# Routing calls of a pipeline step written behind the state update instead of ahead of it

## The chip, the cores and the metric

The kernel runs on one core of a Trainium2 chip. The metric is the device time of one execution, in microseconds. Engines are named as in the profile: PE (TensorE, matmuls and transposes), PEld (its weight loads), DVE (VectorE), ACT (ScalarE), POOL (GpSimd) and SP (SyncE, which issues most DMAs).

## What is computed

Two layers follow each other. The first is a linear attention with a decaying state, per batch and head; the second sends each token to one of eight experts. Cut to what matters, the reference is:

```
for t in range(S):                      # S = 768, head_dim 48, 4 batches, 8 heads
    state = alpha[t, :, None] * state + outer(k[t], v[t])
    y[t]  = q[t] @ state
x = y, one row per token                # 3072 tokens x 384
logits = x @ w_gate + modality_bias[modality_id]      # 8 experts
e_idx  = argmax(logits)
gate_w = softmax(logits)[e_idx]
for e in range(8):
    h = relu(x[e_idx == e] @ w1[e])     # 384 -> 1024
    out[e_idx == e] = gate_w * (h @ w2[e])            # 1024 -> 384
```

Which expert a token goes to is known only once its attention row exists; the kernel sorts the tokens by expert on the core and loads the weights of an expert once it knows that it is wanted.

## The kernel before, in words

**Attention as a pipeline.** The 3072 tokens are cut into 24 units of 128 (a batch has six). A unit passes through five steps of the loop over `s` (lines 797 to 845), and each pass of the loop works on five units at once: `turn_decay`, `decay` and `guard` on unit s, `scale_k` and `scale_q` on unit s-1, `keys` and `scores` on s-2, `combine` on s-3, `outputs`, `rows` and the logits on s-4. A pass is called a step below; there are 27.

`combine` (line 296) is the state's update. On PE it adds into one PSUM bank, tile `y`: the query times the old state (L324), the keys times the values (L330, which gives the new state's increment), and the masked scores times the values (L334). On DVE it then writes the new state S (L338, or L340 in the first unit of a batch), and in the next step the decayed state UB (L304). In the next step ACT copies the same bank out to `yt` (L347, `outputs`). PE needs `yt` for `logits_turned` (L369) and for `rows` (L357), whose result ACT copies to `xs` and SP stores to `xd` in DRAM.

**Routing beside it.** A dictionary `later` holds the routing functions for the step in which they are to be called. The units are taken in groups, `GROUPS = ((0, 6), (6, 12), (12, 16), (16, 18), (18, 22), (22, 24))`. For a group, `route_group` finds each token's expert (a one-hot tile `oh`) on DVE; `route_ranks`, one step later, counts on PE the place of each token within its expert (L453, L457, L461) and turns it into indices on DVE (L465 to L477). The calls fall into steps 10 and 11, 16 and 17, 20 and 21, 22 and 23, 25 and 26, and behind the loop. All of these PSUM results, and those of the logits, share one bank, tile `rt`, so that each waits until the one before has been read.

Two experts are begun early, before all tokens are routed. `route_early` (steps 22 and 24; L539, then L542 to L565) takes the expert with the most tokens so far, and writes its number to `meta` (L545) and a tile `OHE` (L554, L560); `weights` in the same step reads `meta` on SP and loads 3.1 MB of that expert's weights in four DMAs (L656, L658); `early` (steps 23 and 25) finds the tokens with small matmuls of `OHE` (L573), writes their indices (L528 to L533), and gathers their rows from `xd` with two indirect DMAs that POOL issues (L679). In step 25 PE transposes the first expert's gathered rows (`first_inputs`, L118), and from step 26 on it works on that expert's first layer (L111) between the last steps of the attention.

**What sets the order.** Each engine runs its own instructions strictly in the order in which they were put on it. From step 4 on every PE instruction of the loop is pinned to the order in which the Python code writes it (`pin`). On the other engines a scheduler chooses the order when the kernel is built, from what the code writes and its own estimate of when operands are ready; it may put an instruction ahead of one that was written earlier. SP's queue holds the row stores (L363) and the weight loads in one line, POOL's the masks of the scores (L282) and the indirect DMAs.

Behind the loop follow the experts, slot after slot, on PE almost without a pause (L925 to L950).

Of the kernel before, what the change touches and what calls it, by code (L numbers as in the profile page):

```python
# [54 lines left out]
def attention_moe(ctx: ExitStack, tc: tile.TileContext, q, k, v, alpha, mid, wg, mb, w1, w2, out):  # L55
# [49 lines left out]
    def first_layer(j, z, name="tr", bufs=3):  # L105

        if z == 0:
            hps.append(ps.tile([P, 2, T], F32, name=name, bufs=bufs))
        f = 256 * j + P * z
        for d in range(ND):  # L110
            pin(pe.matmul(hps[j][:, z], WR[0][0][:, d, f : f + P], xf[:, d], start=(d == 0), stop=(d == ND - 1)))  # L111

    def first_inputs():
        for d0, d1 in ((0, 2), (2, 3)):
            xp = ps.tile([P, d1 - d0, T], F32, name="sc", bufs=2)
            for d in range(d0, d1):
                for u in range(2):
                    pin(pe.transpose(xp[:, d - d0, u * P : (u + 1) * P], xg[0][:, u, d * P : (d + 1) * P], ident))  # L118
            act.copy(xf[:, d0:d1], xp)

    def pin(ins):

        if mark.get("pin"):
            tc.keep_in_program_order(ins)
        return ins

    def load(i, names="akqv"):
        b, c = divmod(i, NC)
        for n, t in (("a", alpha), ("k", k), ("q", q), ("v", v)):
            if n in names:  # L130
                dst = VT[i % NV][:, :, :D] if n == "v" else nat[n, i % NB][:, :, :D]
                sp.dma_start(dst, t[b, :, c * P : (c + 1) * P, :].rearrange("h t d -> t h d"))
# [97 lines left out]
    def turn_decay(i):  # L230
        pa = trans(i, "a")
        turned = (act.copy if i else vec.tensor_copy)(seg(X[i % 2][:, 1:], 0), pa)
        if i:
            mark["X"] = turned

    def decay(i):
        x, d = X[i % 2], DF[i % 2]
        Fw = sb.tile([P, NP * SEG], F32, name="Fw", bufs=3)
        G = sb.tile([P, NP * SEG + 1], F32, name="G", bufs=4)
        vec.tensor_tensor_scan(  # L240
            G[:, 1:][:, ::-1], x[:, 1:][:, ::-1], DR[:, 1:][:, ::-1], 0.0, op0=ALU.mult, op1=ALU.add
        )
        ac1 = amin[:, i]
        vec.tensor_scalar(ac1, G[:, 1::SEG], AFLOOR, None, op0=ALU.max)
        vec.reciprocal(d[:, 0::SEG], ac1)
        vec.tensor_tensor_scan(Fw, x[:, :-1], d, 0.0, op0=ALU.mult, op1=ALU.add)
        st[i, "G"], st[i, "F"] = G, Fw
# [11 lines left out]
    def scale_k(i):  # L259
        kh = sb.tile([P, NP, P], F32, name="kh", bufs=3)  # L260
        pk = trans(i, "k")
        vec.tensor_tensor(kh, pk, seg(st[i, "G"][:, 1:], 1), op=ALU.mult)
        st[i, "k"] = kh

    def scale_q(i):
        qh = sb.tile([P, NP, P], F32, name="qh", bufs=3)
        pq = trans(i, "q")
        vec.tensor_tensor(qh, pq, seg(st[i, "F"], 1), op=ALU.mult)
        st[i, "q"] = qh
# [15 lines left out]
    def keys(i):  # L285

        kh = st[i, "k"]
        if i % NC < NC - 1:
            p = ps.tile([P, NP, P], F32, name="tr", bufs=3)
            for j in range(NP):  # L290
                pin(pe.transpose(p[:, j], kh[:, j], ident))
            kn = sb.tile([P, NP, P], F32, name="knat")
            act.copy(kn, p)
            st[i, "n"] = kn

    def combine(i):
        c = i % NC
        qh, vt, sc = st[i, "q"], VT[i % NV], st[i, "s"]
        U = UB[i % 2]
        halves = [slice(64 * g, 64 * g + 64) for g in range(2)]  # L300
        if c > 0:
            S0 = st[i, "S"]
            A = st[i, "G"][:, 1::SEG].unsqueeze(2).broadcast_to([P, NP, D])
            vec.tensor_tensor(U[:, :, :D], S0, A, op=ALU.mult)  # L304

        yk = ps.tile([P, 2, 512], F32, name="y")

        def y(r, j):
            return yk[r, j % 2, P * (j // 2) : P * (j // 2 + 1)]

        kv = yk[:, 1, 2 * P : 2 * P + NP * D].rearrange("p (j d) -> p j d", j=NP)
        fresh = {(o, g) for o in range(2) for g in range(2)}

        def first(o, g):
            new = (o, g) in fresh
            fresh.discard((o, g))
            return new

        if c > 0:
            for a in range(2):  # L320
                for o in range(2):
                    for g in range(2):
                        x, j = g ^ o, 2 * a + o
                        pin(pe.matmul(y(halves[x], j), U[halves[g], j], qh[halves[g], j], start=first(o, x), stop=False))  # L324
        if c < NC - 1:
            kn = st[i, "n"]
            for h in range(H):
                j = h // 2
                r = halves[h % 2]
                pin(pe.matmul(kv[r, j], kn[:, j, r], vt[:, h, :D], start=first(1, h % 2), stop=False))  # L330
        for j in range(NP):
            for x, r in enumerate(halves):
                g = x ^ j % 2
                pin(pe.matmul(y(r, j), vt[:, 2 * j + g], sc[g][:, j], start=first(j % 2, x), stop=(j > 1)))  # L334
        if c < NC - 1:
            S1 = sb.tile([P, NP, D], F32, name="S")
            if c > 0:
                vec.tensor_tensor(S1, U[:, :, :D], kv, op=ALU.add)  # L338
            else:
                vec.tensor_copy(S1, kv)  # L340
            st[i + 1, "S"] = S1
        st[i, "yp"] = yk

    def outputs(i):
        yt = sb.tile([P, 2, NP, P], F32, name="yt") if i % 2 == 0 else st[i - 1, "yt"]
        with issue_after("X"):
            act.copy(  # L347
                yt[:, i % 2].rearrange("p (a o) t -> p o a t", o=2),
                st[i, "yp"][:, :, : 2 * P].rearrange("p o (a t) -> p o a t", a=2),
            )  # L350
        st[i, "yt"], st[i, "y"] = yt, yt[:, i % 2]
# [13 lines left out]
    def logits_turned(i):  # L365

        lt = ps.tile([P, 2, P], F32, name="rt")
        for j in range(NP):
            pin(pe.matmul(lt[32 * j : 32 * j + 32], wgp[:, j], st[i, "yt"][:, :, j], start=True, stop=True))  # L369
        l2 = sb.tile([P, 2, P], F32, name="lts")  # L370
        mark["lts"] = act.copy(l2, lt)
        st[i, "l"] = l2

    def logits(i):

        lp = ps.tile([P, 2, P], F32, name="rt")
        for c in range(2):
            pin(pe.transpose(lp[:, c], st[i, "l"][:, c], ident))
        z = slice(i - 1, i + 1)
        vec.tensor_reduce(L[:, z], lp.rearrange("p c (j e) -> p c e j", e=32)[:, :, :E], axis=AX.X, op=ALU.add)  # L380
# [389 lines left out]
    later = {}  # L770
# [26 lines left out]
    for s in range(NU + 3):  # L797
        mark["pin"] = s > 3
        if s > 0 and s + PF - 1 < NU:
            load(s + PF - 1)  # L800
        if s < NU:
            turn_decay(s)
        if 0 <= s - 4:
            outputs(s - 4)
        if s == NU + 1:
            first_inputs()
        if s == NU + 2:
            first_layer(0, 0, "sc", 2)
            first_layer(0, 1)
        if 0 <= s - 1 < NU:  # L810
            scale_k(s - 1)
        if 0 <= s - 1 < NU:
            scale_q(s - 1)
        if s < NU:
            decay(s)
        if 0 <= s - 2 < NU:
            keys(s - 2)
        if s > 4 and s % 2 == 0 and s <= NU:
            logits(s - 5)
        if s > 4 and s % 2:  # L820
            logits_turned(s - 4)
        if 0 <= s - 4:
            rows(s - 4)
        if 0 <= s - 2 < NU:
            scores(s - 2)
        for f, a in later.pop(s, ()):
            f(*a)
        if s < NU:
            guard(s)
        if s == 5:  # L830
            table = bias_table()
            next(table)
        if s == 6:
            next(table, None)
            half_index()
        if s == 4:
            sp.dma_start(xd[MID : MID + 1], zr)
            sp.dma_start(gd[MID : MID + 1], zr[:, 0:1])
        if s == NU:
            out_of_range()  # L840
        if 0 <= s - 3 < NU:
            combine(s - 3)
        if s == NU + 1:
            logits(s - 4)
            route_group(*GROUPS[-2])
# [239 lines left out]
```

## Time and profile before

| what | value |
|---|---|
| median of 3 runs | 410.47 us |
| the three runs | 410.47, 408.89, 410.51 us |
| the profiled execution's own time | 408.91 us |
| its span in the profile | 407.1 us |
| PE busy in the span | 378.2 us (93%) |
| DVE / ACT / POOL busy | 278.2 (68%) / 224.3 (55%) / 137.3 us (34%) |
| attention steps | to about 170 us; experts after that |

The view of waits names who waited for whom and for how long in all. The view by stretches gives the busy time of each engine between two moments, and at the end of its row the mean clock granted to PE (1.00 is full), the share of time in which the 16 DMA engines were busy, and GB/s. The timeline gives start and length in us, engine, line, operation and, in brackets, how long the engine had been idle and who released it; rows that carry one line number and follow each other are merged with their count. DMA queue q1 holds what SP issues, q0 what POOL issues.

### The profile page before, as it was taken

What the parts mean: (1) busy time and instruction counts of PE and PEld (TensorE: products, weight loads), DVE (VectorE), ACT (ScalarE), POOL (GpSimd) and SP (SyncE); (2) the same over time, 40 slices, a digit from 0 to 9 for tenths busy, and PEclk for the clock granted to TensorE, in tenths of its full rate; (3) what the DMA queues carried; (4) which work ended last, traced back from release to release, by engine and by line L of the source; (5) the groups of instructions that cost most, each with busy time, mean ns of one, the idle gap of its engine ahead of it and who ended that gap; (6) DMA issues with size and microseconds to landing.
All of it is one profiled execution on the core that took longest, in us unless ns stands there. A gap on an engine that the chain in (4) does not pass through costs nothing. (4 is left out here: it accounts for less than half of the span.)

```text
span 407.1 us, 9558 instructions
## 1 busy us (share of the span) xinstructions
PE 378.2 (93%) x3659; PEld 347.7 (85%) x3659; DVE 278.2 (68%) x550; ACT 224.3 (55%) x425; POOL 137.3 (34%) x175
## 2 busy tenths in 40 slices
PE   3898999999999888899997999999999999999992
PEld 3777787788778666778997999999999999999992
DVE  6787889878979965587689566665656666554230
ACT  3467677567566435344586657475654656545230
POOL 9321321321222233402657515244351634232010
PEclk9999999999999989999998999999999999999998
DMA  6999988579675096505999786566867657420010
GB/s 129 209 202 214 201 184 192 127 165 199 138 160 117 26 360 210 204 22 163 385 370 331 252 283 202 198 220 203 268 197 264 210 195 238 148 106 35 6 42 10
DMA packets 132655, 75.12 MB, mean 185 GB/s; under 512 B 103777, under 2 KB 120222, under 8 KB 132600
## 3 DMA queue, kind: packets, MB, share of 16 engines
q1 hardware_dynamic: 128504, 64.57, 56.6%
q0 software_dynamic: 4096, 9.85, 7.0%
q8 instruction: 31, 0.51, 0.5%
q14 instruction: 24, 0.20, 0.1%
HBM read 64.95 MB, written 9.65 MB: 183 GB/s over the span
## 5 line engine op out<-in xcount | busy, mean ns | idle before, releaser
L925 PE MATMUL tr<-xH,w1H 128*128 128x256 f32 x264 | 74.7, 286 | 1.3 <-DVE hL L932 1.3
L926 PE MATMUL tr<-xL,w1H 128*128 128x256 f32 x264 | 75.1, 285 | 0.0
L927 PE MATMUL tr<-xH,w1L 128*128 128x256 f32 x264 | 74.9, 285 | 0.0
L282 POOL TENSOR_SCALAR_AFFINE_SELECT scT<-scT 128x512 f32<-128x512 f32 x48 | 35.2, 754 | 107.1 <-ACT scT L281 107.1
L948 PE MATMUL sc<-w2H,hH 128*128 128x384 f32 x192 | 65.4, 342 | 1.0 <-ACT hH L929 1.0
L949 PE MATMUL sc<-w2L,hH 128*128 128x384 f32 x192 | 64.6, 337 | 0.0
L899 DVE TENSOR_TENSOR w2L<-w2r,w2H 128x768 fp32r<-128x768 f32 x52 | 49.1, 956 | 21.9 <-ACT w2H L897 21.0
L950 PE MATMUL sc<-w2H,hL 128*128 128x384 f32 x192 | 63.6, 340 | 0.0
L866 POOL DMA_INDIRECT out_dram<-os,odx x24 | 27.6, 1148 | 89.2 <-ACT os L953 34.9
L899 DVE TENSOR_TENSOR w1L<-w1r,w1H 128x768 fp32r<-128x768 f32 x44 | 41.7, 956 | 21.3 <-ACT w1H L897 20.6
L897 ACT CAST w1H<-w1r 128x768 fp32r<-128x768 f32 x44 | 36.0, 834 | 29.8 <-PE tr L926 23.0
L925 PEld LDWEIGHTS tr<-xH,w1H 128*128 128x128 f32 x264 | 50.9, 194 | 1.6 <-issue 1.6
L926 PEld LDWEIGHTS tr<-xL,w1H 128*128 128x128 f32 x264 | 51.2, 194 | 0.0
L927 PEld LDWEIGHTS tr<-xH,w1L 128*128 128x128 f32 x264 | 51.1, 194 | 0.0
L679 POOL DMA_INDIRECT xg<-xd,idx x26 | 32.0, 1230 | 42.5 <-PE y L887 36.5
L897 ACT CAST w2H<-w2r 128x768 fp32r<-128x768 f32 x52 | 42.2, 834 | 7.0 <-PE sc L950 6.8
L932 DVE SCALAR_TENSOR_TENSOR hL<-tr,hH 128x512 fp32r<-128x512 f32 x46 | 31.5, 686 | 10.5 <-ACT hH L929 7.2
L948 PEld LDWEIGHTS sc<-w2H,hH 128*128 128x128 f32 x192 | 36.1, 188 | 2.4 <-ACT hH L929 1.2
L929 ACT ACTIVATE hH<-tr 128x512 fp32r<-128x512 f32 x46 | 27.4, 595 | 16.2 <-PE tr L927 12.7
L684 POOL DMA_INDIRECT gg<-gd,idx x26 | 30.9, 1187 | 15.8 <-DMA gd<-gs 8.5
L949 PEld LDWEIGHTS sc<-w2L,hH 128*128 128x128 f32 x192 | 36.1, 188 | 0.0
L950 PEld LDWEIGHTS sc<-w2H,hL 128*128 128x128 f32 x192 | 36.0, 188 | 0.0
(218 smaller groups left out, 703.9 us busy)
## 6 DMA issues: line engine op xcount, KB each, us to landing
w1r<-in_moe_w_dram SPq DMA_DIRECT2D x26, 768.0 KB
w2r<-in_moe_w_dram SPq DMA_DIRECT2D x26, 768.0 KB
nat_a<-in_alpha_dram SPq DMA_DIRECT2D x24, 192.0 KB
nat_k<-in_k_dram SPq DMA_DIRECT2D x24, 192.0 KB
nat_q<-in_q_dram SPq DMA_DIRECT2D x24, 192.0 KB
vt<-in_v_dram SPq DMA_DIRECT2D x24, 192.0 KB
xd<-xs SPq DMA_DIRECT2D x24, 192.0 KB
xg<-xd,idx POOLq DMA_INDIRECT x26
```

Of the source, the lines that this page charges most:

```text
L282: pool.affine_select(s, s, [[0, NP], [1, P]], ALU.is_ge, 0.0, base=0, channel_multiplier=-1)
L679: pool.indirect_dma_start(xg[i % NX][:, u], None, xd[0:rows], ix, bounds_check=rows - 1, oob_is_err=False)
L684: pool.indirect_dma_start(gg[i % NX][:, u : u + 1], None, gd[0:rows], ix, bounds_check=rows - 1, oob_is_err=False)
L897: act.copy(hi, src)
L899: vec.tensor_tensor(lw, src, hi.bitcast(F32), op=ALU.subtract)
L925: pe.matmul(hp[:, z], wH[:, d, fs], xH[:, d], start=(d == 0), stop=False)
L926: pe.matmul(hp[:, z], wH[:, d, fs], xL[:, d], start=False, stop=False)
L927: pe.matmul(hp[:, z], wL[:, d, fs], xH[:, d], start=False, stop=(d == ND - 1))
L932: mark[f"h{j}L"] = vec.scalar_tensor_tensor(hL, hp, 0.0, hH.bitcast(F32), op0=ALU.max, op1=ALU.subtract)
L948: pe.matmul(op, hH[:, z, us], wH[:, z], start=(f == 0), stop=False)
L949: pe.matmul(op, hH[:, z, us], wL[:, z], start=False, stop=False)
L950: pe.matmul(op, hL[:, z, us], wH[:, z], start=False, stop=(f == NF - 1))
```

## The change

Two lines move within the loop's body. The call of the routing functions that are due in a step stood between `scores(s - 2)` and `guard(s)`; it now stands behind `combine(s - 3)`. Nothing is added or removed, and no function changes. (`route_ranks` of the last group, which puts ranks and counts into one tile, reads the same in both kernels; so do the calls behind the loop, and the explicit `route_group` of step 25.)

```diff
@@ -823,8 +823,6 @@
             rows(s - 4)
         if 0 <= s - 2 < NU:
             scores(s - 2)
-        for f, a in later.pop(s, ()):
-            f(*a)
         if s < NU:
             guard(s)
         if s == 5:
@@ -840,6 +838,8 @@
             out_of_range()
         if 0 <= s - 3 < NU:
             combine(s - 3)
+        for f, a in later.pop(s, ()):
+            f(*a)
         if s == NU + 1:
             logits(s - 4)
             route_group(*GROUPS[-2])
```

On DVE in step 11, the place where the ranks of the first group are turned into indices (L465 to L477), with the new state S of `combine` (L338), its decayed form (L304), the scaled keys (L262) and the scan of the decay (L240):

```order
+L338 TENSOR_TENSOR S<-UB_154,y 128x192
 L465 TENSOR_TENSOR rk<-rt,oh 128x48
 L473 TENSOR_TENSOR ohs<-ohs,hsum 128x8
+L304 TENSOR_TENSOR UB_160<-S,G 128x4x48
 L467 TENSOR_REDUCE r_209<-rk 128x6
 L474 TENSOR_SCALAR hr<-r_209 128x6
 L475 TENSOR_SCALAR lo<-r_209 128x6
+L262 TENSOR_TENSOR kh<-tr,G 128x512
 L476 SCALAR_TENSOR_TENSOR hi<-m_194,hr 128x6
+L240 SCALAR_TENSOR_TENSOR G<-X_150,DR 128x516
 L477 TENSOR_TENSOR OL<-ioh,lo 128x768
-L338 TENSOR_TENSOR S<-UB_154,y 128x192
```

S, which stood behind all seven routing operations, now stands ahead of the first; UB, the keys and the scan now stand among them. The same holds in steps 17 and 21. In steps 10, 16 and 20, where `route_group` runs, DVE's order does not change at all.

On DVE in step 22, from the reading of the counts for the first early expert (L542) to its number in `meta` (L545), on which SP's weight load waits (L436 to L438 belong to `route_group` of units 16 and 17):

```order
 L542 TENSOR_REDUCE base<-rt 128x1
-L436 SCALAR_TENSOR_TENSOR eq<-ls,rev 128x16
+L304 TENSOR_TENSOR UB_154<-S,G 128x4x48
 L543 SCALAR_TENSOR_TENSOR rest<-rt,base,rev 128x8
-L437 TENSOR_REDUCE m_194<-eq 128x2
+L262 TENSOR_TENSOR kh<-tr,G 128x512
 L544 TENSOR_REDUCE base<-rest 128x1
-L438 TENSOR_TENSOR oh<-eq,m_194 128x16
+L240 SCALAR_TENSOR_TENSOR G<-X_156,DR 128x516
+L268 TENSOR_TENSOR qh<-tr,Fw 128x512
 L545 TENSOR_SCALAR meta<-base 1x1
```

S of this step (L338) now stands directly ahead of L542, but behind `route_group`'s operations and three of the gates (L664 to L666). `meta`, which was written before S, is now written behind S, UB, the keys, the scan and the scaled queries (L268). `OHE` (L554, L560) moves further back still, behind the next scan (L246).

On PE in step 23, where the small matmuls find the tokens of the first early expert (L573):

```order
 L357 MATMUL tr<-ident,yt 128x128 x4
 L277 MATMUL sc<-qh,kh 128x128 x8
+L324 MATMUL y<-qh,UB_154 64x128 x8
+L330 MATMUL y<-vt_104,knat 64x48 x8
+L334 MATMUL y<-scT,vt_104 64x128 x8
 L573 LDWEIGHTS OL
 L573 MATMUL rt<-OHE,OL 128x2
```

The three products of `combine` come ahead of these matmuls and of the ranks that follow them (L453 to L461), instead of behind both and behind the transpose of the gates (L668). The same holds for the ranks and small matmuls in steps 11, 17, 21, 25 and 26. On POOL the gather of the first early expert moves behind both masks of step 23, where it stood between them; SP's order stays.

## The prediction

> **What bounds the kernel now.** I read the view by stretches first, one row for each step of the attention (from one step's L277 on PE to the next), with busy times, granted clock, DMA share and GB/s.
>
> ```profile
> 69.20:75.73 6.53, 6.23 (x95) 5.31 (x94) 6.39 (x16) 3.98 (x9) 1.57 (x2) 1.00 0.63 137
> ...
> 129.56:135.84 6.28, 5.61 (x77) 4.83 (x76) 6.14 (x16) 3.27 (x7) 1.59 (x2) 1.00 0.10 34
> 135.84:143.41 7.57, 6.54 (x94) 5.10 (x93) 7.54 (x30) 3.97 (x9) 1.84 (x2) 1.00 0.19 50
> 143.41:152.94 9.53, 7.83 (x104) 6.66 (x103) 6.47 (x26) 2.95 (x7) 3.88 (x4) 0.82 1.02 374
> 152.94:160.07 7.13, 5.79 (x86) 4.18 (x86) 4.10 (x18) 3.42 (x9) 3.24 (x4) 1.00 0.45 141
> 160.07:170.35 10.28, 9.21 (x139) 7.49 (x138) 5.34 (x23) 2.74 (x7) 5.30 (x6) 1.00 0.81 297
> 170.35:180.00 9.65, 9.65 (x61) 7.95 (x60) 5.97 (x13) 6.20 (x13) 0.00 (x0) 1.00 0.11 36
> ```
>
> PE (first pair behind the length) is the bound: from 170 us on it is full (last row). What can be gained is its idle time in the attention, and that lies in the steps with routing: steps 11 and 21 (first two rows), and above all 22 to 26 (the next four). One of these, step 23, also shows a granted clock of 0.82. The view of PE's waits in steps up to 26 says for whom it waits:
>
> ```profile
> PE rt L369 <- ACT yt L347: 3.7, 7, 1.0
> ...
> PE rt L453 <- DVE vals L529: 1.4, 1, 1.4
> PE tr L357 <- DVE kh L262: 1.4, 3, 0.8
> ...
> PE rt L453 <- issue: 1.1, 1, 1.1
> ...
> PE rt L703 <- DVE rest L543: 0.5, 1, 0.5
> ```
>
> Two kinds: PE waits for `yt` or kh, which come late because S is late on DVE behind routing; or for a routing operand with `combine`, ready to run, queued behind it. The timeline of steps 22 and 23 shows both:
>
> ```profile
> 137.13 0.67 PE L324 MATMUL y<-qh,UB 64*64 64x128 f32 x16
> ...
> 138.23 1.06 PE L334 MATMUL y<-scT,vt 128*64 128x128 f32 x16
> ...
> 139.04 0.56 DVE L436 SCALAR_TENSOR_TENSOR eq<-ls,rev 128x16 f32<-128x16 f32 x1
> ...
> 139.97 0.14 DVE L545 TENSOR_SCALAR meta<-base 1x1 int32<-1x1 f32 x1
> ...
> 141.12 1.01 SPq L656 DMA_DIRECT2D w1r<-in_moe_w_dram  x2
> ...
> 141.24 0.35 DVE L338 TENSOR_TENSOR S<-UB,y 128x192 f32<-128x192 f32 x1
> 141.62 0.59 ACT L347 COPY yt<-y 128x512 f32<-128x512 f32 x1 [1.06 <-DVE S L338]
> ...
> 142.26 0.64 PE L369 MATMUL rt<-yt,wgp 128*32 128x256 f32 x8 [0.99 <-ACT yt L347]
> ...
> 143.64 0.67 DVE L268 TENSOR_TENSOR qh<-tr,Fw 128x512 f32<-128x512 f32 x1
> ...
> 144.51 0.55 PE L573 MATMUL rt<-OHE,OL 128*128 128x2 f16 x16
> 144.65 1.22 DVE L246 TENSOR_TENSOR_SCAN Fw<-X,DF 128x516 f32<-128x516 f32 x1
> ...
> 146.50 0.17 PE L453 MATMUL rt<-oh,tri 128*128 128x16 bf16 x1 [1.44 <-DVE vals L529]
> ...
> 146.68 1.23 POOL L679 DMA_INDIRECT xg<-xd,idx  x1 [0.37 <-DVE vals L529]
> ...
> 148.77 1.94 PE L334 MATMUL y<-scT,vt 128*64 128x128 f32 x16
> ...
> 150.64 0.84 PE L227 MATMUL tr<-ident,nat_k 128*128 128x128 f32 x4
> ...
> 157.21 0.88 PE L118 MATMUL sc<-ident,xg 128*128 128x128 f32 x6
> ```
>
> The last product of `combine` ends at 139.29, but S starts at 141.24 and `yt` right behind it, so L369 waits. In step 23 the reading of L573's result (L529) stands behind the scan L246 on DVE, L453 waits 1.44 us for it, and `combine` behind L453; its L334 then takes 1.94 us where step 22's took 1.06. The reason is the clock. PE's row is the first pair again:
>
> ```profile
> 144.40:147.80 3.40, 1.70 (x40) 1.13 (x36) 3.28 (x18) 1.33 (x3) 2.11 (x2) 0.98 1.02 377
> 147.80:151.05 3.25, 3.25 (x38) 2.84 (x35) 0.38 (x2) 0.00 (x0) 1.77 (x3) 0.50 1.06 379
> 181.90:185.30 3.40, 2.05 (x12) 1.55 (x11) 3.37 (x19) 0.00 (x0) 0.00 (x0) 1.00 0.00 0
> 185.30:188.70 3.40, 3.40 (x22) 3.37 (x21) 2.11 (x7) 0.00 (x0) 0.00 (x0) 1.00 0.20 12
> ```
>
> After 3.4 us with PE busy half the time the clock is 0.50 for 3.25 us, which costs about 1.6 us; after 60% busy it stays at 1.00. So the stall of step 23 costs about 3 us with what follows it.
>
> **The change part by part.** Work is only reordered, so each term is a difference of start times. I give them in the old trace's clock.
>
> *Steps 11, 17, 21.* S leaves the place behind the indices. Above: all of PE's idle time there, 0.30 in step 11 (17 is its twin) and 0.67 in step 21, 1.3 in sum. Below: nothing, because DVE is busy 6.39 of 6.53 us there and gets no less work; if kh or the scan is then late, PE waits for it instead. kh now passes two of the seven operations, but DVE must idle until S is possible. I take a little over half, 0.8.
>
> *Step 22.* Ahead of S stay L436 to L438 and the gates' L664 to L666, which wait for an exponential on ACT; the operations of `route_early` go behind. From L436's end at 139.60, with about 0.2 us (an estimate) for each of the six links left, S starts near 140.85 instead of 141.24, and PE's L369 and L357 follow: 0.35.
>
> *Step 23.* `combine` now runs straight behind the scores: L277 at 143.05, 1.1 for itself (143.41 to 144.51) and 2.1 for the three products (137.13 to 139.29): done at 146.2. L573 needs OHE, which DVE now writes behind the scan. qh starts at 143.5; the scan stood 1.0 behind that, and 0.6 more for the small operations now between: 145.2, and OHE near 146.6. L573 runs 146.7 to 147.3, L529 and L453 near 147.7, the gates' transpose near 148.4, and the next step's first transpose at 148.65 instead of 150.64. The waits left are 0.5, 0.4 and 0.5; a stretch of 3.4 us around them is some 2.0 us busy, nearer to the row that kept its clock (2.05) than to the one that lost it (1.70). With the next L277 at 150.7 instead of 152.94 the step gains 2.25 less the 0.35 above: 1.9. Bounds: 0.3 if the clock falls all the same, 3.3 if no wait is left.
>
> *Step 24 and the early expert.* L703's 0.5 goes, and L369's 0.83 behind `yt` (S no longer stands behind `route_early`): with 1.1 + 0.15 + 2.15 + 0.15 of work before it, L118 could start at 154.3, and the next L277 at 156.35 instead of 160.07. That is 1.5 on top. But `meta` (L545) now stands behind S, UB, kh, the scan and qh: from 139.97 to about 144.1. The weight DMAs move 4.1 us back, while the gather moves only from 146.68 to about 147.7, so the two now meet. The rows stored next on SP wait behind the weights, as the gates' store does; nobody on PE needs them before step 26. The DMA view, packets and MB of each queue; first 142 to 151.4 us, then 151.4 to 153.4, then 194.5 to 195.5, 195.5 to 197, and last the quarter us to 153.0, the last with q1 packets of the gates' store, with the timeline's row of the POOL instruction that waited for it:
>
> ```profile
> q1 hardware_dynamic: 1881, 3.19, 97.6%
> ...
> q0 software_dynamic: 128, 0.39, 49.0%
> q1 hardware_dynamic: 155, 0.16, 22.7%
> ...
> q1 hardware_dynamic: 133, 0.20, 54.9%
> q0 software_dynamic: 59, 0.20, 50.5%
> ...
> q1 hardware_dynamic: 389, 0.60, 105.8%
> ...
> q1 hardware_dynamic: 3, 0.00, 1.1%
> ...
> 153.84 1.01 POOL L684 DMA_INDIRECT gg<-gd,idx  x1 [3.95 <-DMA gd<-gs]
> ```
>
> In step 23 the gather (q0, 0.39 MB) moved only when the 3.1 MB of weights were through; near 195 one gather of 0.20 MB got half of the engines between two weight DMAs, with more weights moving behind it. I read that as turns of one DMA each. At 2.0 us for each weight DMA the four would end near 149.3, 151.3, 153.3 and 155.3; the gather's two halves, issued to 150.2, take the turns at 151.3 and about 153.6; with 1.0 us for a half at half share, as near 195, and 0.8 until the waiting engine starts (153.0 to 153.84), L118 starts near 155.4. Cost 1.1, so 0.4 remains of 1.5. Bounds: no cost at all, or a gather behind all weights (below). The weights themselves are needed at L111, which stands behind that L277 at 156.35, three products and L573 (1.1 + 2.1 + 0.6): not before 160, some 4 us after they land.
>
> *Steps 25 and 26.* L453 no longer waits 1.07 us for `oh` ahead of `combine`; L378 will wait some 0.4 for the `rt` bank. 0.65.
>
> *Behind.* From 170.35 on PE is full, so the shift is carried to the end. Sum: 0.8 + 0.35 + 1.9 + 0.4 + 0.65 = 4.1 us. The profiled execution took 408.91 us (a span of 407.1 and 1.8 around it), so 404.8; the median shown is 1.56 above that execution, so I forecast **406.4**. A measurement of this kernel tells about 0.5%, 2 us, from no change.
>
> **One rule against the trace.** The Trainium skill (TensorE: Matmul & The Clock Gate, "What's actually happening") says that the clock halves after at least one idle window of about 3.4 us. The width agrees with the 3.25 us at 0.50; but here a window that was busy for half of it sufficed. By the Trainium skill's rule nothing of step 23's loss would be the clock's, and the sum would be 4.1 - 1.6 = 2.5; the row at 0.50 speaks against it already, so it gets no chance of its own.
>
> **Rivals.**
>
> *The gather is not held.* DMA engines share as soon as a gather is there, as near 195; then L118 starts at 154.3, the gain is 5.2, the time 405.3. Against it: 151.4 to 153.4, where it came only behind the weights. The Trainium skill (DMA: Bandwidth & Descriptors, "Queues, rings and completion order") has this rule: an engine takes turns between queues packet by packet, some 9 to 17 descriptors each. No row here shows turns that short.
>
> *Slower: the early expert's gather comes behind all its weights.* Place: L118, pinned ahead of all later PE work. The weights end 4.1 later, at 155.5; the gather takes 2.0 us more, as it did; with the same 0.8 L118 starts at 158.3, a wait of 4.0, and the clock halves for 3.4 us, 1.7. Step 24 then gives 1.5 - 5.7 = -4.2 and the sum is -0.5: 411.0, and 412.6 if step 23's clock falls too. It decides once L118 starts later than about 157.8. For it: the rows of 151.4 to 153.4. Against it: 194.5.
>
> *Little comes of it.* DVE, busy 7.54 of 7.57 us in step 22, limits the steps, so the first two terms are nil, and step 23's waits still halve the clock (0.3): 0.3 + 0.4 + 0.65 = 1.35, 409.1. In steps 10, 16 and 20 the change indeed moves nothing on DVE.
>
> **How the numbers follow.** Forecast 0.42, gather not held 0.20, slower 0.18, little 0.18, anything else 0.02. The forecast's own range is 405.2 to 408.0. To leave out no more than 2 in 10 the range goes to 404.2 below (gather not held, all of the first term) and 410.8 above (most of the slower case). Faster by over 0.5%, below 408.4: 0.42 + 0.20 and a little of the third, 0.64. Slower by over 0.5%: the far half of the slower case and the rest, 0.10. Within: 0.26.
>
> **What would show it.** Right: granted clock 1.00 through step 23, S starting within 0.3 us of L334's end in steps 11, 17, 21 and 23 to 25, no wait of L453 ahead of `combine`, steps 23 and 24 near 7.6 and 6.8 us, L118 waiting about 1 us for the gather. Wrong: a wait of L118 above 3 us with a half clock behind it; a clock of 0.50 behind L453; L357 waiting for kh where it waited for `yt`; or a gain in the steps that is gone at 170 us.

## The result

The changed kernel takes 406.59 us (median of 20 runs), the kernel before 410.49 us (20 runs). The ratio is 0.9927, with a 95% interval of 0.9901 to 0.9953: some 3.0 us faster (1.9 to 4.1). In a later series the ratio was 0.9892 (0.9839 to 0.9944). Runs more than 1.5% above the fastest of the same kernel are left out of all ratios, one profile of the changed kernel that fell into such a run is not used, and whether its second profile, a single run of 410.68 us, is one can't be told. The forecast was 406.4 us, a gain of 4.1 us: the direction came out as forecast, and the size lies at the upper end of the interval. Inside, the sum is wrong in two places, in opposite directions: up to step 24 the change gained 1.7 us more than forecast, and from step 24 on it lost 2.6 us where a gain of 1.05 was forecast, as the table below shows.

The profiled execution of the changed kernel took 406.9 us, with a span of 405.2 us. Its view by stretches, for steps 11, 21, 22, 23 and 24 and for the time from step 25's L277 to the next group of L111 (columns as in the rows shown of before):

```profile
69.31:75.23 5.92, 5.92 (x95) 5.25 (x94) 4.96 (x15) 3.83 (x9) 1.34 (x2) 1.00 0.66 145
...
128.24:133.69 5.45, 5.45 (x77) 4.76 (x76) 5.12 (x15) 3.27 (x7) 1.60 (x2) 1.00 0.12 39
133.69:141.21 7.52, 6.54 (x94) 5.02 (x93) 7.38 (x24) 3.85 (x9) 2.15 (x2) 1.00 0.08 28
141.21:148.37 7.16, 6.20 (x104) 5.34 (x103) 6.84 (x33) 2.95 (x7) 4.42 (x4) 1.00 0.49 163
148.37:156.73 8.36, 5.97 (x87) 4.33 (x86) 2.65 (x19) 3.48 (x9) 1.28 (x3) 0.96 1.06 368
156.73:168.66 11.93, 11.61 (x139) 9.77 (x138) 2.77 (x16) 2.74 (x7) 7.23 (x8) 0.74 0.87 298
```

Step 11 falls from 6.53 to 5.92 us, step 21 from 6.28 to 5.45, step 23 from 9.53 to 7.16 at full clock. Step 22 stays (7.57 to 7.52). Step 24 grows from 7.13 to 8.36 us, and behind it the clock is 0.74 on average, where it was 1.00. What PE waits for says why (the view of PE's waits in the changed kernel, steps up to 26):

```profile
PE sc L118 <- DMA xg<-xd,idx: 2.4, 2, 2.0
...
PE rt L369 <- ACT yt L347: 1.7, 4, 0.6
...
PE tr L357 <- DVE kh L262: 0.6, 1, 0.6
PE rt L573 <- DVE OHE L560: 0.4, 1, 0.4
...
PE rt L453 <- DVE vals L529: 0.3, 1, 0.3
```

The waits for `yt` fell from 3.7 to 1.7 us, those for kh from 1.4 to 0.6, and L453's 1.4 us to 0.3. A new one is at the top: L118, the transposes of the gathered rows of the first early expert. The timeline of the changed kernel around it:

```profile
142.22 0.13 DVE L545 TENSOR_SCALAR meta<-base 1x1 int32<-1x1 f32 x1
...
143.36 1.01 SPq L656 DMA_DIRECT2D w1r<-in_moe_w_dram  x2
...
145.69 0.17 PE L453 MATMUL rt<-oh,tri 128*128 128x16 bf16 x1 [0.32 <-DVE vals L529]
145.86 1.24 POOL L679 DMA_INDIRECT xg<-xd,idx  x1 [0.53 <-DVE vals L529]
147.41 1.02 POOL L679 DMA_INDIRECT xg<-xd,idx  x1 [0.30 <-issue]
...
153.90 0.30 PE L118 MATMUL sc<-ident,xg 128*128 128x128 f32 x1 [2.03 <-DMA xg<-xd,idx]
...
154.55 0.76 PE L118 MATMUL sc<-ident,xg 128*128 128x128 f32 x5 [0.35 <-DMA xg<-xd,idx]
...
155.81 0.98 PE L357 MATMUL tr<-ident,yt 128*128 128x128 f32 x4
```

The rows are asked for at 145.86 and 147.41 us and are there at 153.9 and 154.5. Behind the wait L357 takes 0.98 us where it otherwise takes 0.60 to 0.66. The windows of the clock, of the changed kernel (granted clock third from the end):

```profile
149.20:152.60 3.40, 2.67 (x57) 2.09 (x55) 0.97 (x5) 1.51 (x3) 1.22 (x2) 1.00 1.06 389
152.60:156.00 3.40, 1.75 (x16) 1.01 (x17) 1.62 (x14) 1.02 (x4) 0.00 (x0) 1.00 1.05 359
156.00:159.30 3.30, 3.30 (x32) 2.74 (x35) 0.00 (x0) 1.27 (x4) 1.66 (x2) 0.50 0.95 279
159.30:162.70 3.40, 3.40 (x49) 2.74 (x42) 0.03 (x1) 0.66 (x2) 1.56 (x3) 0.50 1.08 393
```

A stretch in which PE was busy 1.75 of 3.40 us is followed by 6.7 us at half clock. What step 23 no longer loses, steps 24 to 26 lose now.

**Where the time went.** The table sets two stretches of every profile beside each other: A from step 10's L277 to step 24's L277, B from there to the last L453 (ranks of the last group, near 178 us). It is worked out from the starts of these instructions in the timeline; the clock is that granted in stretch B.

| kernel | A, us | B, us | A + B | clock in B |
|---|---|---|---|---|
| before | 90.38 | 26.71 | 117.1 | 1.00 |
| before, second profile | 90.15 | 25.65 | 115.8 | 1.00 |
| changed | 85.51 | 29.57 | 115.1 | 0.88 |
| changed, second profile | 85.58 | 27.98 | 113.6 | 0.94 |
| steps 11, 17, 21 alone | 88.50 | 25.58 | 114.1 | 1.00 |
| step 23 alone | 87.50 | 25.24 | 112.7 | 1.00 |
| first expert's choice stays | 85.58 | 25.17 | 110.8 | 1.00 |
| L118 late | 85.85 | 24.84 | 110.7 | 1.00 |
| L118 late, second profile | 86.07 | 28.28 | 114.4 | 0.94 |
| weights behind the gather | 85.63 | 24.15 | 109.8 | 1.00 |
| wait filled with work | 85.86 | 26.16 | 112.0 | 1.00 |
| choice stays and L118 late | 85.96 | 24.83 | 110.8 | 1.00 |

The change gains 4.7 us in A (mean 90.27 against 85.55) and loses 2.6 in B (26.2 against 28.8). The net, 2.1 us, agrees with the two profiled spans first compared (407.1 and 405.2). Each row of the table is one execution. Ahead of A and behind B executions of one and the same program differ by more than that (last section), so the causes below are read from A and B, and the ratios are given beside them.

### The profile page after: what moved, and what is told of

The parts are those of the page before. It is cut to its first block, busy times and chain, and to the rows that moved or that the text cites. A ratio compares the mean times of both kernels' runs of the same rounds, so it can differ in the third digit from the quotient of the medians.

```text
span 405.2 us, 9558 instructions
## 1 busy us (share of the span) xinstructions
PE 378.9 (94%) x3659; PEld 349.0 (86%) x3659; DVE 272.8 (67%) x550; ACT 224.1 (55%) x425; POOL 136.0 (34%) x175
```

## Experiments

Where an experiment adds lines to the program, the line numbers behind them are higher by as many; the text keeps the old ones.

### The ranks of steps 11, 17 and 21 alone

Of the kernel before, only the calls of these three steps move:

```diff
-        for f, a in later.pop(s, ()):
-            f(*a)
+        calls = later.pop(s, ())
+        behind = [(f, a) for f, a in calls if s in (11, 17, 21)]
+        for f, a in calls:
+            if (f, a) not in behind:
+                f(*a)
...
             combine(s - 3)
+        for f, a in behind:
+            f(*a)
```

> Only the ranks of steps 11, 17 and 21 (route_ranks of the first groups, with the gates of step 17) are called behind combine; all other routing calls stay where they were before. Theory A (from the two profiles): S, no longer queued behind the indices on DVE, frees two links of the chain in each of these steps, so steps 10 to 12, 16 to 18 and 21 shorten by about 0.8 us each, 2.45 in sum, and since nothing behind them changes the time falls by 2.0 to 2.5 us. Theory B (as predicted): the gain cannot exceed PE's idle time in these steps, 1.3 us, and is 0.8 in sum. Theory C: the steps shorten by 2.45, but the stall of step 23 (clock 0.50 behind L453) falls into another window of the clock, so that the end moves by 1.6 less or more than the steps do.

Measured: 405.7 us beside 408.77 us of before, ratio 0.9952 (0.99 to 1.0005). Steps 11, 17 and 21 take 6.16, 5.92 and 5.44 us; before, 6.53, 6.52 and 6.28: 1.8 us less. Stretch A is 1.8 us shorter. The ratio alone, whose interval reaches 1, would not decide; by the steps the bound of 1.3 us is broken, so B of the expectation is wrong; A named 2.45, which counted steps 10 and 16 in. These vary without any change there (16: 6.26 us here, 6.70 in another kernel with the same order, 6.70 and 6.64 in the two profiles of before). C did not occur.

The bound was PE's idle time. The timeline of before and then of the changed kernel in step 11, from the last transposes to L357, shows what that leaves out:

```profile
74.49 0.38 PE L378 MATMUL rt<-ident,lts 128*128 128x128 f32 x2
75.17 0.63 PE L357 MATMUL tr<-ident,yt 128*128 128x128 f32 x4 [0.30 <-DVE kh L262]
```

```profile
74.48 0.38 PE L378 MATMUL rt<-ident,lts 128*128 128x128 f32 x2
74.70 0.60 PE L357 MATMUL tr<-ident,yt 128*128 128x128 f32 x4
```

Without a wait L357 starts 0.22 us after L378 starts, 0.16 before L378's record ends; with the wait it starts 0.68 after it. A wait whose idle time is 0.30 thus costs 0.46, since consecutive matmuls overlap and a wait takes the overlap away.

One more thing stands in this run, step 22, by stretch and by PE's waits:

```profile
135.88:143.79 7.91, 6.54 (x94) 5.09 (x93) 7.88 (x31) 3.97 (x9) 2.15 (x2) 1.00 0.23 50
```

```profile
PE rt L539 <- DVE L L380: 0.7, 1, 0.7
```

With step 21 shorter and step 22 in its old order, step 22 takes 7.91 us instead of 7.57: L539 stands ahead of `combine` and waits for DVE. In the changed kernel step 22 has 7.52. The change of step 22's own order is thus worth 0.39 us, but step 21's earlier end takes 0.34 of it.

### Step 23 alone

The same edit with `if s == 23`.

> Only the calls of step 23 (tokens of the first early expert with its gather, ranks and gates of units 16 and 17) stand behind combine; steps 11, 17, 21, 22, 24 and 25 are as before. Theory A: step 23 falls from 9.53 to about 7.3 us with the clock at 1.00 and no wait of L453 ahead of combine; with the weights as early as before L118 does not wait, and step 24 has 7.1 us or less: the time is 2 to 3.5 us below before. Theory B: the gain of step 23 came from step 22's order (OHE and the scan there); L453 or L573 still waits over 1 us, the clock falls, and the time is within 1 us of before. Theory C: L118, reached 2.2 us earlier, waits for the gather also with early weights, and over half of the gain is lost there.

Measured: 404.91 us, ratio 0.9908 (0.986 to 0.9956). Steps 23 and 24 of this kernel by stretches, then two of PE's waits in it:

```profile
144.70:151.44 6.74, 6.13 (x104) 5.34 (x103) 6.14 (x26) 2.95 (x7) 3.78 (x4) 1.00 1.04 384
151.44:158.00 6.56, 5.66 (x87) 4.09 (x86) 2.77 (x19) 3.48 (x9) 2.95 (x5) 1.00 0.79 280
```

```profile
PE sc L118 <- DMA xg<-xd,idx: 0.4, 1, 0.4
...
PE rt L453 <- DVE vals L529: 0.3, 1, 0.3
```

Step 23 falls from 9.5 to 6.74 us at full clock. That is 0.4 below the changed kernel, because OHE is written in time when step 22 keeps its order. L118 waits 0.4 us, not 2.4, although PE comes to it earlier than before. Theory A holds, with a little more gained than it named and that wait of 0.4; the move of this one step gives a ratio like that of the whole change.

### The first expert's choice and weights stay

As the changed kernel, but `route_early(0)` and `weights(0)` of step 22 keep the old place:

```diff
+        calls = later.pop(s, ())
+        behind = [(f, a) for f, a in calls if not (f in (route_early, weights) and a[0] == 0)]
+        for f, a in calls:
+            if (f, a) not in behind:
+                f(*a)
```

> As the changed kernel, but in step 22 the choice of the first early expert and its weight loads (route_early and weights of expert 0) stay at the old place, between scores and guard. Theory A: the wait of L118 (2.4 us in the changed kernel) comes from meta, written 2.2 us later, whose weight DMAs then meet the gather. With meta near 138 us the weights end before 150 us, the gather lands before L118 is reached, L118 waits less than 0.5 us, the clock stays at 1.00 in steps 24 to 26, and the time is 3 to 6 us below the changed kernel: 400.5 to 403.5 where that has 406.6. Theory B: the gather is slow by itself (issued late by POOL, six us from issue to landing); L118 still waits 1.5 us or more and the time stays within 1 us of the changed kernel.

Measured: 403.93 us, ratio 0.9908 (0.9862 to 0.9953). From the timeline of this kernel:

```profile
154.00 0.30 PE L118 MATMUL sc<-ident,xg 128*128 128x128 f32 x1
...
155.25 0.77 PE L118 MATMUL sc<-ident,xg 128*128 128x128 f32 x5 [0.95 <-DMA xg<-xd,idx]
```

L118 waits once, 0.95 us, the clock stays at 1.00 to the end of B, and B is 25.17 us. The wait is less than with late weights but above the 0.5 expected. The DMA view of this kernel from 151.0 to 151.5 us and from 152.0 to 152.5, and POOL's issue of the gather, show where the rest comes from:

```profile
q1 hardware_dynamic: 123, 0.18, 104.2%
...
q0 software_dynamic: 44, 0.17, 82.7%
q1 hardware_dynamic: 57, 0.05, 27.8%
...
147.97 1.24 POOL L679 DMA_INDIRECT xg<-xd,idx  x1 [0.76 <-DVE vals L529]
```

Here too the gather (q0) stood behind the weights (q1): it began to move between 151.5 and 152.0 us, as they ended, some 3.8 us after its issue. By the stretches B of the expectation is wrong (A + B is 4.3 us below the changed kernel's first profile, 2.8 below its second); the ratios of the two kernels, 0.9908 and 0.9927, can't be told apart.

### L118 later in its step

As the changed kernel, with the gather exactly as late, but PE has the work of step 25 up to `combine` ahead of L118:

```diff
-        if s == NU + 1:
-            first_inputs()
...
             combine(s - 3)
+        if s == NU + 1:
+            first_inputs()
```

> As the changed kernel, but in step 25 the transposes of the gathered rows (L118) are written behind combine instead of at the start of the step, so that PE has some 4 us of other work before it needs the gather; meta, weights and gather stay as late as in the changed kernel. Theory A: the gather lands at about 153.9 us whatever PE does, so the wait of 2.4 us and the half clock behind it (two windows, 3.3 us) both go: steps 24 to 26 shorten by 4 to 5 us in all, the time is 401.5 to 403.5. Theory B: the clock falls for another reason (steps 24 and 25 hold too little work for PE), then only the wait goes and the time is 404 to 405. Theory C: what is behind L118 (the first layer, L111) comes late by as much, and the time is that of the changed kernel, 406 to 407.

Measured: 403.21 us, ratio 0.9889 (0.984 to 0.9939). Step 24 and the time behind it, by stretches:

```profile
149.97:155.57 5.60, 4.66 (x80) 3.51 (x80) 2.26 (x17) 2.67 (x7) 1.27 (x3) 1.00 1.05 387
155.57:165.54 9.97, 9.65 (x145) 8.21 (x144) 4.12 (x20) 3.53 (x10) 5.60 (x7) 1.00 1.02 344
```

No wait of L118, step 24 takes 5.60 us without it, clock 1.00 throughout B, B 24.84. Theory A holds.

### The wait filled with work

The wait and the half clock go together in all runs so far. Here only the half clock is taken away: PE does 16 transposes that nothing reads, ahead of L118.

```diff
             xp = ps.tile([P, d1 - d0, T], F32, name="sc", bufs=2)
+            if d0 == 0:
+                for _ in range(16):
+                    pin(pe.transpose(xp[:, 0, :P], ident, ident))
```

> As the changed kernel, but PE does 16 transposes of the identity matrix, which nothing reads, directly ahead of L118 (about 1.9 us of work, by 0.88 us for the six of L118), so that it is busy while the gather is awaited; the gather is as late as in the changed kernel. Theory A: what L118's wait costs is the wait itself (2.4 us) and two windows at half clock behind it (3.3 us). With the wait filled the clock stays at 1.00 and only the wait remains: steps 25 and 26 shorten by about 3.3 us and the time is 402.5 to 404. Theory B: the half clock has another cause (the phase of the windows, or the weights of the second early expert that begin to move then); the time is that of the changed kernel, 406 to 407, or up to 0.5 us more.

Measured: 406.25 us beside 408.41, ratio 0.9909 (0.9875 to 0.9942). The timeline, and the stretches of step 24 and of the time behind it:

```profile
156.29 1.94 PE L118 MATMUL sc<-ident 128*128 128x128 f32 x16
158.07 0.27 PE L121 MATMUL sc<-ident,xg 128*128 128x128 f32 x1
158.69 0.77 PE L121 MATMUL sc<-ident,xg 128*128 128x128 f32 x5 [0.35 <-DMA xg<-xd,idx]
```

```profile
152.93:160.55 7.62, 7.27 (x103) 5.80 (x102) 2.66 (x19) 3.49 (x9) 1.27 (x3) 1.00 1.06 375
160.55:169.81 9.26, 8.94 (x138) 7.52 (x138) 3.75 (x16) 2.76 (x8) 6.37 (x7) 1.00 1.03 351
```

The gather is about as late as in the changed kernel (the last wait for it ends 8.3 us after POOL's issue, there 8.7, and L118's real transposes, here L121, begin 1.8 us late), but the clock is 1.00. B is 26.16 us: 3.4 below the changed kernel's first profile with two windows at half clock, 1.8 below its second with one. So the half clock follows PE's idleness, not the weights that begin to move then. This is one profile; in the whole table B has a clock below 1.00 only where PE waited 1.8 us or more at one place. The time does not show it: 406.25 us misses the 402.5 to 404 of A and lies where B had it, and the ratio can't be told from the 0.9927 of the change.

### Weights behind the gather

As the changed kernel, but SP issues the weights of the first expert behind the row store of step 24, 7 us later:

```diff
-        sp.dma_start(xd[row(i) : row(i) + P, :], xs)
+        mark["xs", i] = sp.dma_start(xd[row(i) : row(i) + P, :], xs)
...
+    def weights_behind(i, w):
+        with tc.issue_after(mark["xs", 20].ins):
+            weights(i, w)
...
-            at(z + 2, weights, e, e)
+            at(z + 2 if e else z + 4, weights_behind if e == 0 else weights, e, e)
```

> As the changed kernel, but the four weight DMAs of the first early expert are issued on SP behind the row store of step 24 (some 6 us later than in the changed kernel), so that the gather's rows move while no weights do. Theory A: in the changed kernel the gather lay between the weight DMAs; with the engines free it lands within 5.5 us of POOL's issue, at about 151.5 us on the changed kernel's clock, L118 does not wait, the clock stays at 1.00 in steps 24 to 26, and the first layer (L111) does not wait for the weights: 401.5 to 404. Theory B: the gather needs eight us by itself (from issue to landing, as in the changed kernel); L118 waits 1.5 us or more, and the time is 405 to 407. Theory C: the weights are then too late for L111, which waits over 2 us for them: 405 or more.

Measured: 405.51 us beside 408.41, ratio 0.9939 (0.99 to 0.9979). The DMA view of the changed kernel from 151.0 to 151.5 us, and that of this kernel from 147.5 to 148.0 (packets, MB, share of 16 engines):

```profile
q0 software_dynamic: 28, 0.09, 51.3%
q1 hardware_dynamic: 55, 0.08, 48.9%
```

```profile
q0 software_dynamic: 13, 0.06, 67.2%
q1 hardware_dynamic: 3, 0.00, 1.0%
```

Alone, the gather begins to move some 2 us after its issue at 145.78, and L118 starts at 151.64 with no wait. In the changed kernel its first packets move between 150.0 and 150.5, some 4.3 us after the issue, and from 150.5 to 153.5 it shares the engines with the weights. The collision is shown. But the gain does not come out at the end: with the weights 7 us later the first expert's second layer starts late. The timeline of this kernel on PE, near 175 us:

```profile
174.92 0.44 PE L952 MATMUL sc<-w2H,hH 128*128 128x384 f32 x1 [1.67 <-DVE hL L936]
...
176.29 0.53 PE L954 MATMUL sc<-w2H,hL 128*128 128x384 f32 x1
```

and the clock is lowered there too (0.53 us for a matmul that takes 0.33 at full clock). What hL waits for is, by the profile, a row store; SP issues the row stores of the last steps behind the weights of both experts. In the same view on DVE:

```profile
174.17 1.29 DVE L936 SCALAR_TENSOR_TENSOR hL<-sc,hH 128x512 fp32r<-128x512 f32 x2 [2.66 <-DMA xd<-xs]
```

From the last L453 to the last matmul it takes 220.9 us against 218.3 in kernels whose clock holds. A of the expectation is right on the gather and wrong on the time. L111 did not wait, so C is wrong too: the price is paid, as far as the profile names the cause, by the stores queued behind the weights.

### Both kernels again, and the two remedies together

Second profiles of the changed kernel and of the kernel before:

> The changed kernel a second time, for its steps. Theory A: L118 waits 2 us or more again and the clock is 0.50 in part of the 8 us behind it, so that step 10's start to the last L453 takes 114 to 115.5 us as in the first profile (115.1). Theory B: whether the clock falls there depends on where the windows of 3.4 us happen to lie in an execution; then the clock stays at 1.00 in this one and the same stretch takes about 112 us.

> The kernel before a second time, for its steps. The wait of 1.07 us of L453 in step 25, which the profile puts down to nothing that it shows, is absent in both kernels of this study that kept that order. If it was chance, step 10's start to the last L453 takes about 116.2 us instead of 117.1; the half clock behind step 23's L453 (step 23 of 9.5 us) comes again. If it belongs to the kernel, the stretch takes 117.1 again.

The changed kernel took 410.68 us in that one run, the kernel before 406.99; step 10 started at 66.63 and 63.63 us. A and B are in the table. L118 waited 2.4 us again, as A of the expectation has it, but A + B is 113.6 us, below the 114 that it named, since this time one window fell to half clock, not two. The stretches of the second profile of the changed kernel show it:

```profile
154.70:158.10 3.40, 1.31 (x19) 0.88 (x15) 2.31 (x17) 0.59 (x1) 0.64 (x2) 1.00 1.05 372
158.10:161.40 3.30, 3.00 (x17) 1.85 (x17) 0.14 (x1) 1.23 (x3) 0.25 (x1) 0.50 1.02 302
161.40:164.80 3.40, 3.40 (x66) 2.71 (x64) 0.00 (x0) 1.61 (x4) 2.97 (x4) 0.99 0.98 362
```

In the kernel before, L453's 1.07 us in step 25 did not come again, and B is 25.65: that wait does not belong to the kernel. Step 23's stall came again, at 9.60 us with a clock of 0.82.

Then, on another chip, the changed kernel, the one with late L118, and one that has both that edit and the choice of the first expert at the old place:

> The changed kernel, beside the next two on the same chip. In two profiles its steps up to the start of step 24 were 4.7 us shorter than before, and steps 24 to 26 some 2.6 us longer, together 2.1 us faster. Theory A: a ratio to before of 0.993 to 0.995. Theory B: the start of the kernel, where loads decide, differs by more than that from one execution to the next, and the ratio lies outside.

> The changed kernel with L118 behind combine, a second time, beside the changed kernel. Theory A: the profiles say 4.0 us between the two (from step 24's start to the last L453: 24.8 us against 28.0 to 29.6); ratio to before 0.984 to 0.989, some 3 to 4.5 us below the changed kernel. Theory B: part of the gain is given back behind 180 us, then 1 to 2.5 us below the changed kernel.

> Both remedies: the choice of the first early expert and its weight loads stay at the old place in step 22, and L118 stands behind combine in step 25. Theory A: each takes away the same wait, so together they bring what one brings: step 23 is 0.4 us shorter (OHE is early, L573 does not wait) and step 22 0.4 longer (L539 waits for L380), the ratio to before is 0.984 to 0.990. Theory B: with early weights and late transposes the gather no longer matters and the first layer can start earlier; 1 us or more below the kernel with late transposes alone.

| kernel | median, us | ratio to before (411.01 us) |
|---|---|---|
| changed | 408.06 | 0.9892 (0.9839 to 0.9944) |
| L118 late | 404.57 | 0.9852 (0.9809 to 0.9895) |
| choice stays and L118 late | 403.18 | 0.9798 (0.9752 to 0.9843) |

The changed kernel's ratio lies below the 0.993 to 0.995 of its A, though the interval reaches into it; late L118 is 3.5 us faster than the changed kernel, as its A had it. Both remedies together have the lowest ratio of all, 2.0% below before (1.6 to 2.5); its interval still meets that of late L118 alone. Their median is 1.4 us below that kernel's, as B had it, but in the profiles they bring no more than one of them (A + B 110.8 against 110.7), as A had it, so this is not decided. The second profile of the kernel with late L118 however has a wait of 2.1 us of L378 for L529 in step 25, with half clock behind it (B 28.28), which its first profile and that of both remedies lack. Its timeline there:

```profile
160.37 0.16 DVE L528 TENSOR_SCALAR idx<-rt 128x2 int32<-128x2 f32 x1 [2.25 <-remote]
...
160.65 0.47 PE L378 MATMUL rt<-ident,lts 128*128 128x128 f32 x2 [2.09 <-DVE vals L529]
```

DVE's L528 stands idle 2.25 us there for something that the profile puts on no engine; what it was is open, and whether the better ratio of the two remedies comes from it too.

## Why the prediction was right, and where it was not

**What bounds the kernel** was read rightly: the gain lay in S, `yt` and L453's stall. Behind the last L453 the first two profiles take the same (219.7 and 219.6 us), so the shift is carried to the end there; the second two differ by more than the change (218.3 and 221.1), because the clock fell near 220 us in one of them. The sum is another matter. Up to step 24 (stretch A) a gain of 3.05 us was forecast and 4.7 measured, behind it (B) a gain of 1.05 was forecast and a loss of 2.6 measured. The two errors offset each other only in part: the profiles leave 2.1 us and the ratio 3.0 of the 4.1 forecast. That the median of 406.59 us lies 0.2 us from the forecast is luck. Its steps, with before's two profiles against the changed kernel's:

*Steps 11, 17, 21: forecast 0.8 us, at most 1.3; measured 1.8* (19.3 us for the three, then 17.5 and 17.6), and the same alone. S starts within 0.1 us of the last product's end, as forecast. Wrong was the upper bound, in two ways. Idle time was taken for the cost of a wait: each of the three waits cost about 0.16 us more, because the overlap of neighbouring matmuls goes too. From L378's start to L357's it took 0.68, 0.68 and 1.05 us, and in the first profile now 0.22, 0.41 and 0.32, which is 1.5 us less in sum; what is left above 0.22 is kh, a little late in steps 17 and 21. And the ranks on PE were left out: ahead of the products they held these back by 0.2 to 0.3 us a step, behind them they delay the next transposes by 0.1 to 0.2, which makes the remaining 0.3. (The 4.7 us of stretch A hold another 0.5 in steps 10 and 16, 13.2 us for both before and 12.7 now, where nothing moved on DVE and kernels of one order differ by as much.)

*Step 22: forecast 0.35; measured 0.05.* The new order is worth something (0.39 by the first experiment), but step 21's earlier end consumed it; the prediction had set step 22 against an unchanged start. S starts 5.40 us behind the step's L277 in both kernels (141.24 less 135.84, 139.09 less 133.69), and DVE is busy 7.38 of 7.52 us: in this one step the rival that little comes of it, because DVE limits, was right.

*Step 23: forecast 1.9, measured 2.4.* The reason held: L453 waits 0.32 us, the clock stays at 1.00, the half-clock window is gone. The term was undersized: the three waits left are 0.35, 0.32 and 0.29 us, where 0.5, 0.4 and 0.5 were taken.

*Step 24 and the early expert: forecast a gain of 0.4 with a wait of 1.1 us at L118; measured a loss of 1.2 in the first profile and 2.5 in the second (9.43 us against 6.96), with a wait of 2.4 in both.* Late `meta` and the meeting of gather and weights were forecast and are shown. To set the rest against the prediction, both are counted from step 23's L277, at 143.05 us in the prediction and 141.21 in the trace, since the steps ahead of it move `meta` and the gather as well as PE. PE was ready for L118 after 10.7 us (153.90 less 2.03, less 141.21), where the prediction had 11.25 (154.3); the last wait for the gather ended after 13.3 us (154.55), where it had 12.35 (155.4). The second profile has 10.65 and 13.35. So PE came 0.6 us earlier than forecast, as step 23 took 7.16 us where 7.65 was forecast, and the gather came 1.0 us later than the turns gave. In the second profile the whole window of half clock lies within this step.

*Turns of one DMA each* is wrong: from 150.5 to 153.5 us the gather and the weights moved in every half microsecond together. (The row of 389 packets that the prediction gives for 195.5 to 197 us is that of 193.0 to 194.5; the right one has 383 packets and 0.57 MB, which changes nothing in the reading.) The Trainium skill (DMA: Bandwidth & Descriptors, "Queues, rings and completion order") has turns of some 9 to 17 descriptors; sharing as fine as in the row at 151.0 agrees with turns shorter than a DMA, but does not show their length. It does not explain why the gather, which moves some 2 us after its issue when alone, started only after some 4.3 us, nor why with early weights it started only as these ended; that is open.

*Steps 25 and 26: forecast a gain of 0.65; measured a loss of 1.6 in the first profile and a gain of 0.1 in the second* (step 25's L277 to the last L453: 19.58 and 18.69 before, 21.21 and 18.55 now). The forecast rested on a wait of 1.07 us that one profile showed and the second did not. What it missed is the half clock: the slower rival had it behind a wait of 4.0 us at L118, the forecast's own case had none; a wait of 2.4 sufficed, as the window at 152.60 shows (1.75 of 3.40 us busy, next to the 1.70 that lost its clock before). So the outcome is the forecast's case with a good part of the slower rival's mechanism. That the gather would stand behind all weights, as this rival had it, did not occur, nor did the rival without a hold.

*The clock's rule.* The Trainium skill (TensorE: Matmul & The Clock Gate, "What's actually happening") asks for an idle window of about 3.4 us. Here 1.75 of 3.40 busy, and in the second profile 1.31 of 3.40, were followed by a clock of 0.50; the filled wait shows that the idleness between is what does it. The prediction was right to go by the row.

## What to carry to other kernels

When a chain moves forward, look for the first instruction on it that waits for something that does not move with it, here a DMA gather: what is gained on the chain behind the gather's trigger ends there, and the wait can cost twice over when the clock falls behind it. Give such an instruction other work ahead of it in program order, and keep the trigger of long DMAs (the choice of the weights) at its early place while the rest moves. And price a wait on PE at a little more than its idle time, and take no term from a wait that only one profile shows.

## What the runs showed of the hardware that was not expected

The half clock lasts one or two windows for the same wait: 3.3 us after 1.31 of 3.40 us busy, 6.7 us after 1.75 of 3.40. In the longer case PE was busy without a pause in the first window at half clock, and the second followed all the same. The Trainium skill (TensorE: Matmul & The Clock Gate, "What's actually happening") says that the windows run freely and do not start with the work; that a like wait gave one window here and two there agrees with it, but it does not explain the second window, and that is open.

Executions of one program differ mostly outside the part that was changed: step 10 started between 62.4 and 67.1 us in the profiles of this study, and from the last L453 to the last matmul it took 218.2 to 218.3 us where the clock held and 219.6 to 221.1 where it fell near 176 or 220 us. Together that is more than the change is worth.
